# One chunk table changed: when the second weight is loaded, summed and rounded, and when three activations are queued, in a linear-attention block with a gated feed-forward

## The chip, the cores and the metric

The kernel is one program on one core of a Trainium2 chip. Its engines are TensorE (PE in the profile; PEld is its loading of weights), VectorE (DVE), ScalarE (ACT), GpSimd (POOL) and SyncE (SP), whose queue issues every DMA that is spoken of here. The metric is the device time of one execution in microseconds (us). Before the change it is 1128.17 us, the median of three runs (1127.15 to 1129.49).

## The reference, cut to what matters

```python
xn = layernorm(x)                       # x: 2048 x 576, float32
q, k, v = split(xn @ wqkv)              # 32 heads of 18
s = linear_attention(phi(q), phi(k), v) @ wo
h = gelu(xn @ w1 + b1)                  # w1: 576 x 4608
g = silu(h @ w2 + b2)                   # w2: 4608 x 576
out = x + s * g
```

## The kernel before, in words

Every float32 matmul is done with pairs: an operand is rounded to a short form (`hi`, a CAST on ScalarE), and what the rounding lost is kept beside it (`lo`, a subtraction on VectorE); three matmuls, hi by hi, hi by lo and lo by hi, make one product. The two matmuls of the feed-forward are besides done with seven products of blocks where eight would be plain (a Strassen-Winograd scheme), so that weights and activations first have sums made of their quarter blocks, and then those sums are rounded.

Attention takes the first 283 us or so and is not touched. The feed-forward runs over two halves of the rows (`half`), each over nine chunks of 512 columns of the hidden layer (`c`; `step` counts the 18 chunks). **A chunk has 28 steps** (`NS`). Steps 0 to 6 and 7 to 13 are the seven products of two `Up` objects: x by the first weight, in the order 1, 2, 6, 5, 7, 3, 4 (`UP`). Steps 14 to 27 are the seven products by the second weight, in the order 1, 2, 7, 4, 5, 3, 6 (`ORDER`), two steps each. In the first half of the rows every chunk prepares its weights while TensorE works, and stores them to DRAM; the second half loads them ready. The last chunk is done plainly.

TensorE, VectorE, ScalarE and GpSimd run the feed-forward strictly in the order in which it is written (`in_order`), SP's queue is placed by the scheduler. What is written where is set by tables: `add(base + k, f)` puts work behind step k of a chunk, `at_step` calls it there.

- **`P1` and `P0`** are the steps for the first weight of the chunk's second `Up` (steps of its own chunk) and of the next chunk's first `Up` (steps of the chunk before). `T` are GpSimd's sums in the raw weight (lines 800 to 807, tile `w1raw`), `hi` the roundings (line 811) and `lo` what is left (line 816), for the tiles `wa`, `w` (product 6), `wc` and `wd`.
- **`PW2`** is the same for the second weight: `T` are the four sums 5, 7, 6, 4 in the raw tile `w2raw` (line 1151), `hi` and `lo` the seven operands (lines 754 and 757, tiles `w2_...`, printed by the profile as `w__` and a number). Sum 5 overwrites the block that operand 1 reads, sum 6 the one of operand 3, and sum 4 the one of operand 2, so each comes behind those roundings.
- **`load_raw`** (line 609) loads the next chunk's raw second weight into the one `w2raw` buffer.
- **`Up.step`**: bank `a` is written by product 1, read by a ScalarE copy into `mid` (line 1107), then added to by product 6, read again (line 1114), added to by product 7. TensorE therefore waits at step 2 and step 9 for the copy of line 1107, and at step 4 and step 11 for that of line 1114. VectorE's additions are on lines 1110 to 1129, the gelu on line 1098.
- **`silu_first`** (line 1309) applies silu to a finished block of the first half of the rows, in place in `macc`, and stores it (`c_dram`); the blocks C12, C21 and C22 are queued at steps 0 and 1 of the first chunk of the second half, behind the additions `combine` (line 1249).

Of the kernel before, what the change touches and what calls it, by code (L numbers as in the profile page):

```python
# [44 lines left out]
def linear_attention_gated_ffn(ctx, tc, x, xT, wqkv, wo, w1, w1e, b1, w2, b2, out):  # L45
# [733 lines left out]
    class W1:  # L779
# [11 lines left out]

        def T(self, i):


            a, b = slice(0, 2), slice(2, 4)
            f0, f1, src = self.f0, self.f1, self.src
            tt = EW1.tensor_tensor
            if i == 5:
                src[5] = f0[:, a]
                tt(src[5], f1[:, a], f0[:, a], op=SUB)  # L800
            elif i == 6:
                src[6] = w1p.tile([P, 2, P], F32, tag="w1t6", name="w1t6", bufs=1)
# [153 lines left out]
    def beside(i, k):  # L956
# [14 lines left out]
        else:  # L971
# [91 lines left out]
    C11, C12, C21, C22, U1 = range(5)  # L1063
# [69 lines left out]
    class W2:  # L1133
# [9 lines left out]

        def T(self, i):
            src = self.src
# [22 lines left out]
        def load(self, i):  # L1168
            t, self.ops[i] = op_tile(fr, [2, HD], f"w2_{i}", 1, f"w2_{self.n}_")
            nc.sync.dma_start(t.bitcast(F32), w2_dram[self.n % NC, i])  # L1170

    class HOps:
# [6 lines left out]
        def add(self, pr, g):  # L1179
            for (par, b), t in g.items():  # L1180
                self.A[pr, b, par] = t
                self.src[{(0, 0): 1, (0, 1): 2, (1, 1): 4, (1, 0): "-"}[b, par], pr] = t
# [218 lines left out]
    NS = 28  # L1401

    def plan_w1(add, w, base, T, hi, lo):
        for table, what in ((T, w.T), (hi, w.hi), (lo, w.lo)):
            for i, at in table.items():
                add(base + at, what, i)

    P1 = dict(  # L1410
        T={5: 1, 6: 1, 7: 1, 4: 2},
        hi={"a": 0, 6: 2, "c": 3, "d": 4},
        lo={"a": 0, 6: 3, "c": 4, "d": 5},
    )
    P0 = dict(
        T={5: 24, 6: 24, 7: 25, 4: 25},
        hi={"a": 21, 6: 25, "c": 26, "d": 27},
        lo={"a": 22, 6: 25, "c": 26, "d": 27},
    )


    PW2 = dict(
        T={5: 3, 7: 3, 6: 4, 4: 4},
        hi={2: 0, 1: 1, 3: 2, 7: 5, 4: 6, 5: 8, 6: 9},
        lo={2: 1, 1: 2, 3: 3, 7: 6, 4: 7, 5: 9, 6: 10},
    )
    W2_NEXT = {1: 15, 2: 17, 7: 19, 4: 21, 5: 23, 3: 25, 6: 27}
    PH = dict(
        S={(7, 0): 7, (5, 0): 8, (6, 0): 11, (3, 0): 11, (7, 1): 13, (5, 1): 14, (6, 1): 15, (3, 1): 15},
        hi={  # L1430
            (1, 0): 7, (2, 0): 9, (7, 0): 10, (1, 1): 11, (2, 1): 12, (7, 1): 15, (4, 0): 16,
            (4, 1): 17, (5, 1): 18, (5, 0): 19, (6, 0): 20, (3, 0): 21, (3, 1): 22, (6, 1): 23,
        },
        lo={
            (1, 0): 10, (2, 0): 10, (7, 0): 11, (1, 1): 12, (2, 1): 13, (7, 1): 15, (4, 0): 16,
            (4, 1): 17, (5, 1): 18, (5, 0): 19, (6, 0): 20, (3, 0): 21, (3, 1): 22, (6, 1): 23,
        },
# [22 lines left out]
    for step in range(n_chunks):  # L1460
        half, c = divmod(step, NC)
        base = step * NS
        plain = step == n_chunks - 1
        h = HOps(c)
        if half == 0:
            plan_w1(add, w1t[2 * step + 1], base, **P1)
            for what in ("T", "hi", "lo"):
                for i, at in PW2[what].items():
                    add(base + at, getattr(w2t[step], what), i)
        change = step == NC - 1  # L1470
        if not plain:
            add(base + (11 if change else 7), load_we, 2 * step + 2)
            add(base + (16 if change else 14), load_we, 2 * step + 3)
        if half == 0 and c < NC - 1:
            add(base + 0, make, W1, w1t, 2 * step + 2)
            add(base + 4, make, W1, w1t, 2 * step + 3)
            add(base + 1, lambda n=2 * step + 2, base=base: plan_w1(add, w1t[n], base, **P0))
            make(W2, w2t, step + 1)
            add(base + 22, w2t[step + 1].load_raw)
        elif not plain:  # L1480
            add(base + (11 if change else 7), make, W1Loaded, w1t, 2 * step + 2)
            add(base + (11 if change else 14), load_six, 2 * step + 2)
            add(base + (16 if change else 14), make, W1Loaded, w1t, 2 * step + 3)
            if step + 2 < n_chunks:
                make(W2, w2t, step + 1)
                for i, at in W2_NEXT.items():
                    add(base + at + 10 * change, lambda i=i, n=step + 1: w2t[n].load(i))
            else:
                make(W2, w2t, step + 1)

                w = w2t[step + 1]
                add(base + 7, w.load_raw)
                for f in range(CF):
                    add(base + 22 + f, lambda f=f, w=w: (w.plain(f), w.hi(("p", f))))
                    add(base + 24 + f, w.lo, ("p", f))
        if not plain:
            if half == 0 and c == NC - 1:
                for k, at in X_AT.items():
                    add(base + at, load_x_part, k)
                add(base + 14, lambda: x_new.update(rs=load_rests(0)))  # L1500
                add(base + 25, silu_first, C11)
                for k in range(2):
                    add(base + 26 + k, combine, C12, nc.vector, slice(2 * k, 2 * k + 2))
                    add(base + 26 + k, combine, C21, nc.gpsimd, slice(2 * k, 2 * k + 2))
            for what in ("S", "hi", "lo"):
                for (i, pr), at in PH[what].items():
                    add(base + at, getattr(h, what), i, pr)
        if half == 1 and c == 0:
            add(base, silu_first, C12)
            add(base, silu_first, C21)  # L1510
            add(base, combine, C22, nc.vector, slice(0, 2))
            add(base + 1, combine, C22, nc.vector, slice(2, 4))
            add(base + 1, silu_first, C22)
        if half == 1 and c:
            for k in range(2):
                tiles = {}
                def load(k=k, t=7 + c, tiles=tiles):
                    tiles[0] = finish_tiles(k)
                    finish_load(t, k, tiles[0])
                add(base, load)  # L1520
                add(base + 4, lambda k=k, t=7 + c, tiles=tiles: finish(t, k, tiles[0]))
        if plain:
            for m in (C12, C21, C22):
                add(base + 4, combine, m, nc.gpsimd)
            for t, at in enumerate((6, 7, 12, 13, 5, 12, 12, 12)):
                add(base + at, load_xs, t)
            for b, f, at, lo in (
                (0, 0, 7, 8), (0, 1, 8, 9), (1, 0, 10, 10), (1, 1, 10, 11), (0, 2, 11, 12),
                (0, 3, 12, 13), (1, 3, 13, 13), (1, 2, 13, 13),
            ):  # L1530
# [68 lines left out]
```

## Time and profile before

| | us |
|---|---|
| runs before, median of 3 | 1128.17 |
| the profiled execution | 1128.05 |
| its span, first to last instruction | 1126.3 |
| attention, to the start of the feed-forward | 282.66 |
| first half of the rows, first chunk's `Up` | 24.60 |
| the eight chunk lengths from 307.26 to 689.46 | 382.20 |
| first half to second half, 689.46 to 738.80 | 49.34 |
| a chunk of the second half | 44.65 |

The page's first part gives the busy time of the engines, the fourth the chain of work that ended last. A stretch by stage (busy time of each engine, with the clock granted to TensorE as PEclk) and a timeline of instructions (start, length, engine, line, tiles, and in brackets the idle time ahead with what ended it) are the other two views used below.

### The profile page before, as it was taken

What the parts mean: (1) busy time and instruction counts of PE and PEld (TensorE: products, weight loads), DVE (VectorE), ACT (ScalarE), POOL (GpSimd) and SP (SyncE); (2) the same over time, 40 slices, a digit from 0 to 9 for tenths busy, and PEclk for the clock granted to TensorE, in tenths of its full rate; (3) what the DMA queues carried; (4) which work ended last, traced back from release to release, by engine and by line L of the source; (5) the groups of instructions that cost most, each with busy time, mean ns of one, the idle gap of its engine ahead of it and who ended that gap; (6) DMA issues with size and microseconds to landing.
All of it is one profiled execution on the core that took longest, in us unless ns stands there. A gap on an engine that the chain in (4) does not pass through costs nothing.

```text
span 1126.3 us, 18080 instructions
## 1 busy us (share of the span) xinstructions
PE 1098.3 (98%) x6702; PEld 1012.0 (90%) x6702; DVE 774.1 (69%) x1096; ACT 551.5 (49%) x954; POOL 461.9 (41%) x394
## 2 busy tenths in 40 slices
PE   9999999999999999999999999899999999999998
PEld 8999989999798897988879798798998998989988
DVE  7655348787788787888778887474574664745756
ACT  6454355555745556464554645544244253352542
POOL 3433224333646546375463745224232242241340
PEclk9999999999999999999999999999999999999999
DMA  6864224675947648375583839978676767766452
GB/s 209 212 149 125 72 84 152 200 260 185 365 172 269 228 182 312 145 304 200 192 302 151 327 133 354 377 269 273 215 228 220 248 205 226 222 226 209 144 189 86
DMA packets 84224, 242.78 MB, mean 216 GB/s; under 512 B 11430, under 2 KB 23718, under 8 KB 81448
## 3 DMA queue, kind: packets, MB, share of 16 engines
q1 hardware_dynamic: 84136, 241.62, 63.0%
q8 instruction: 53, 0.87, 0.3%
q14 instruction: 35, 0.29, 0.1%
HBM read 145.66 MB, written 93.99 MB: 213 GB/s over the span
## 4 chain that ended last, share of the span: by engine, by line
PE 87%; POOL 5%; issue 2%; ACT 2%; DVE 2%; DMA 1%; SPq 0%; POOLq 0%; ACTq 0%; DVEq 0%
PE pm L1233 34%; PE a L1090 12%; PE e L1090 8%; PE bc L1090 6%; PE pk L320 6%; PE pq L320 5%; PE ps_s L730 5%; PE pv L320 4%; POOL w2raw L1151 4%; PE pd L1349 2%; PE ps_kva L381 1%; DMA op_c<-wc 1%; PE ptp L712 1%; POOL w1t L803 1%; DMA b2b<-b 1%
## 5 line engine op out<-in xcount | busy, mean ns | idle before, releaser
L1239 DVE TENSOR_TENSOR macc<-pm,macc 128x576 f32<-128x576 f32 x218 | 164.6, 755 | 62.6 <-PE pm L1233 61.3
L754 ACT CAST h_h<-g 128x512 fp32r<-128x512 f32 x204 | 122.9, 620 | 136.3 <-PE pm L1233 135.3
L757 DVE TENSOR_TENSOR h_l<-g,h_h 128x512 fp32r<-128x512 f32 x204 | 157.9, 778 | 11.8 <-ACT h_h L754 11.5
L1199 POOL TENSOR_TENSOR mid<-g 128x512 f32<-128x512 f32 x34 | 44.1, 1296 | 107.3 <-ACT g L1098 107.2
L1098 ACT ACTIVATE g<-bc,b1c 128x512 f32<-128x512 f32 x72 | 49.6, 689 | 55.9 <-DVE bc L1110 39.3
L1193 POOL TENSOR_TENSOR g<-g 128x512 f32<-128x512 f32 x34 | 52.3, 1538 | 39.8 <-ACT h_h L754 20.2
L1107 ACT COPY mid<-a 128x512 f32<-128x512 f32 x36 | 21.1, 585 | 95.2 <-PE a L1090 94.0
L800 POOL TENSOR_TENSOR w1raw<-w1raw 128x256 f32<-128x256 f32 x18 | 13.3, 738 | 130.6 <-ACT h_h L754 68.9
L1151 POOL TENSOR_TENSOR w2raw<-w2raw 128x576 f32<-128x576 f32 x36 | 65.2, 1810 | 2.1
L1120 DVE TENSOR_TENSOR z<-a,mid 128x512 f32<-128x512 f32 x36 | 25.0, 695 | 51.0 <-PE a L1090 51.0
L1196 POOL TENSOR_TENSOR g<-g 128x512 f32<-128x512 f32 x34 | 52.6, 1548 | 7.6 <-DVE h_l L757 5.5
L1321 POOL TENSOR_TENSOR fin1l<-fin1h,fin1l 128x288 f32<-128x288 f32 x8 | 7.0, 878 | 118.7 <-DMA fin1l<-s_dram 56.9
L1110 DVE TENSOR_TENSOR bc<-bc,mid 128x512 f32<-128x512 f32 x36 | 25.0, 694 | 41.7 <-PE bc L1090 39.8
L1090 PE MATMUL a<-s,w 128*128 128x512 f32 x108 | 32.1, 438 | 17.5 <-ACT mid L1107 17.5
L1190 POOL TENSOR_TENSOR g<-g 128x512 f32<-128x512 f32 x34 | 47.5, 1398 | 2.7
L1121 ACT COPY mid<-a 128x512 f32<-128x512 f32 x36 | 21.1, 587 | 50.0 <-DVE z L1120 50.0
L695 POOL TENSOR_TENSOR pbuf<-phiq,den 128x576 f32<-128x576 f32 x16 | 19.4, 1212 | 63.6 <-DVE den L694 63.6
L1090 PEld LDWEIGHTS a<-s,w 128*128 128x128 f32 x108 | 21.6, 207 | 25.6 <-ACT mid L1107 21.3
L320 PE MATMUL pk<-wkv_h,xh 128*128 128x288 f32 (+1 forms) x160 | 38.2, 321 | 0.4 <-ACT xh L247 0.4
L320 PE MATMUL pk<-wkv_l,xh 128*128 128x288 f32 (+1 forms) x160 | 38.2, 321 | 0.0
L339 DVE SCALAR_TENSOR_TENSOR phik<-pk,ek 128x576 f32<-128x576 f32 x16 | 12.1, 758 | 37.0 <-ACT ek L337 37.0
L730 PE MATMUL ps_s<-kw_h,th 128*128 128x288 f32 x160 | 35.5, 303 | 0.0
(894 smaller groups left out, 3671.1 us busy)
## 6 DMA issues: line engine op xcount, KB each, us to landing
we<-we_dram SPq DMA_DIRECT2D x36, 448.0 KB
w2raw<-w SPq DMA_DIRECT2D x10, 1152.0 KB
w1raw<-w SPq DMA_DIRECT2D x18, 512.0 KB
op_a<-wa SPq DMA_DIRECT2D x18, 512.0 KB
op_c<-wc SPq DMA_DIRECT2D x18, 512.0 KB
op_d<-wd SPq DMA_DIRECT2D x18, 512.0 KB
wc<-op_c SPq DMA_DIRECT2D x18, 512.0 KB
wa<-op_a SPq DMA_DIRECT2D x18, 512.0 KB
```

Source lines behind the costliest of these rows:

```text
L320: nc.tensor.matmul(ps[:, h, : ws.stop - ws.start], st, w[:, k, ws], start=(begin and i == 0), stop=(end and i == len(seq) - 1), skip_group ...
L730: nc.tensor.matmul(ps[:, h, :HD], st[:, k, :], w[:, k, h * HD : (h + 1) * HD], start=(i == 0), stop=(i == len(seq) - 1),)
L754: nc.scalar.copy(pair[0], src)
L757: eng.tensor_tensor(pair[1], src, pair[0].bitcast(F32), op=SUB)
L1090: nc.tensor.matmul(ps, st, mv, start=first and n == 0, stop=n == len(seq) - 1, skip_group_check=True,)
L1098: nc.scalar.activation(g, ps, AF.Gelu_apprx_tanh, bias=b1c[:, f : f + 1])
L1151: tt(dst, a, b, op=SUB)
L1190: tt(src[5, pr], A(1, 0), A(1, 1), op=ADD)
L1193: tt(src[6, pr], src[5, pr], A(0, 0), op=SUB)
L1196: tt(src[3, pr], A(0, 1), src[6, pr], op=SUB)
L1233: nc.tensor.matmul(ps[:, q, :HD], hs[p][st][:, cs], m[:, p, :], start=(n == 0 and i not in CHAIN), stop=(n == 5), skip_group_check=True,)
L1239: nc.vector.tensor_tensor(dst, src, dst, op=ADD)
```

## The change

`P1`, `P0` and `PW2` get other step numbers; `PW2` may now hold negative ones, which are steps at the end of the chunk before, and a new function `plan_w2` queues those from the chunk before; the load of the next raw second weight is queued at step 16 instead of 22; and the three `silu_first` are queued together behind step 13 of their chunk.

```diff
     P1 = dict(
-        T={5: 1, 6: 1, 7: 1, 4: 2},
-        hi={"a": 0, 6: 2, "c": 3, "d": 4},
-        lo={"a": 0, 6: 3, "c": 4, "d": 5},
+        T={5: 1, 6: 1, 7: 3, 4: 3},
+        hi={"a": 0, 6: 4, "c": 7, "d": 7},
+        lo={"a": 0, 6: 5, "c": 8, "d": 8},
     )
     P0 = dict(
-        T={5: 24, 6: 24, 7: 25, 4: 25},
+        T={5: 18, 6: 18, 7: 19, 4: 19},
...
     PW2 = dict(
-        T={5: 3, 7: 3, 6: 4, 4: 4},
+        T={5: -1, 7: 2, 6: 2, 4: 4},
...
+    def plan_w2(n, ahead):
+        for what in ("hi", "lo", "T"):
+            for i, at in PW2[what].items():
+                if (at < 0) == ahead:
+                    add(max(n * NS + at, 0), getattr(w2t[n], what), i)
...
-            add(base + 22, w2t[step + 1].load_raw)
+            add(base + 16, w2t[step + 1].load_raw)
+            plan_w2(step + 1, True)
...
         if half == 1 and c == 0:
-            add(base, silu_first, C12)
-            add(base, silu_first, C21)
             add(base, combine, C22, nc.vector, slice(0, 2))
             add(base + 1, combine, C22, nc.vector, slice(2, 4))
-            add(base + 1, silu_first, C22)
+            for m in (C22, C21, C12):
+                add(base + 13, silu_first, m)
```

GpSimd, in the `Up` of the chunk with raw weights `w1raw6`, `w1raw7` and `w2raw3` (one chunk of the first half; the others read alike). Before:

```order
L807 TENSOR_TENSOR w1raw6_4219<-w1raw6_4219,w1t6_4631 128x256
L800 TENSOR_TENSOR w1raw7_4292<-w1raw7_4292 128x256
L803 TENSOR_TENSOR w1t6_4723<-w1raw7_4292 128x256
L805 TENSOR_TENSOR w1raw7_4292<-w1raw7_4292 128x256
L807 TENSOR_TENSOR w1raw7_4292<-w1raw7_4292,w1t6_4723 128x256
L1151 TENSOR_TENSOR w2raw3_4590<-w2raw3_4590 128x576 x4
```

With the change:

```order
L807 TENSOR_TENSOR w1raw6_4230<-w1raw6_4230,w1t6_4530 128x256
L1151 TENSOR_TENSOR w2raw3_4483<-w2raw3_4483 128x576
L800 TENSOR_TENSOR w1raw7_4287<-w1raw7_4287 128x256
L803 TENSOR_TENSOR w1t6_4734<-w1raw7_4287 128x256
L1151 TENSOR_TENSOR w2raw3_4483<-w2raw3_4483 128x576 x2
L805 TENSOR_TENSOR w1raw7_4287<-w1raw7_4287 128x256
L807 TENSOR_TENSOR w1raw7_4287<-w1raw7_4287,w1t6_4734 128x256
L1151 TENSOR_TENSOR w2raw3_4483<-w2raw3_4483 128x576
```

The first sum of the second weight stands ahead of all of `w1raw7`, two more stand amid them, and only the last is still at the end.

VectorE, from the last addition of a chunk's products (line 1239) to the addition of product 2 in the next (line 1110). Before:

```order
L1239 TENSOR_TENSOR macc_3214<-pm6_4672,macc_3214 128x2x288
L816 TENSOR_TENSOR wd_6_4686<-w1raw6_4219,wd_6_4686 128x512
L816 TENSOR_TENSOR wa_7_4703<-w1raw7_4292,wa_7_4703 128x512
L1110 TENSOR_TENSOR bc6_4693<-bc6_4693,mid_3217 128x512
L757 TENSOR_TENSOR w2_3__4708<-w2raw3_4590,w2_3__4708 128x576
```

With the change:

```order
L1239 TENSOR_TENSOR macc_3214<-pm6_4674,macc_3214 128x2x288
L757 TENSOR_TENSOR w2_3__4669<-w2raw3_4483,w2_3__4669 128x576
L816 TENSOR_TENSOR wd_6_4694<-w1raw6_4230,wd_6_4694 128x512
L816 TENSOR_TENSOR wa_7_4711<-w1raw7_4287,wa_7_4711 128x512
L757 TENSOR_TENSOR w2_3__4688<-w2raw3_4483,w2_3__4688 128x576
L1110 TENSOR_TENSOR bc6_4698<-bc6_4698,mid_3217 128x512
```

Two subtractions of the second weight, those of operands 1 and 3, now stand ahead of the addition of line 1110.

ScalarE, from the gelu of step 6 to that of step 8. Before:

```order
L754 CAST w2_3__4798<-w2raw3_4590 128x576
L1098 ACTIVATE g_4808<-bc6_4693,b1c_78 128x512
L754 CAST w2_3__4810<-w2raw3_4590 128x576
L1107 COPY mid_3217<-a7_4815 128x512
L754 CAST h10_h_4833<-g_4720 128x512
L1098 ACTIVATE g_4844<-bc7_4817,b1c_78 128x512
```

With the change:

```order
L754 CAST w2_3__4793<-w2raw3_4483 128x576
L1098 ACTIVATE g_4803<-bc6_4698,b1c_78 128x512
L754 CAST w2_3__4805<-w2raw3_4483 128x576
L1107 COPY mid_3217<-a7_4810 128x512
L811 CAST wc_7_4822<-w1raw7_4287 128x512
L811 CAST wd_7_4824<-w1raw7_4287 128x512
L754 CAST h10_h_4832<-g_4731 128x512
L1098 ACTIVATE g_4843<-bc7_4812,b1c_78 128x512
```

The rounding just ahead of the copy of line 1107 reads GpSimd's last sum (4) before, and the last but one (6) with the change; the two roundings of `wc` and `wd`, which stood at steps 3 and 4, follow the copy, and their subtractions on VectorE (line 816) follow the addition of step 8.

More of the change, by code (lines that the diff above doesn't have):

```diff
@@ L1410, in linear_attention_gated_ffn @@
     P1 = dict(
-        T={5: 1, 6: 1, 7: 1, 4: 2},
-        hi={"a": 0, 6: 2, "c": 3, "d": 4},
-        lo={"a": 0, 6: 3, "c": 4, "d": 5},
+        T={5: 1, 6: 1, 7: 3, 4: 3},
+        hi={"a": 0, 6: 4, "c": 7, "d": 7},
+        lo={"a": 0, 6: 5, "c": 8, "d": 8},
     )
     P0 = dict(
-        T={5: 24, 6: 24, 7: 25, 4: 25},
-        hi={"a": 21, 6: 25, "c": 26, "d": 27},
-        lo={"a": 22, 6: 25, "c": 26, "d": 27},
+        T={5: 18, 6: 18, 7: 19, 4: 19},
+        hi={"a": 16, 6: 23, "c": 25, "d": 27},
+        lo={"a": 17, 6: 24, "c": 26, "d": 28},
     )
     PW2 = dict(
-        T={5: 3, 7: 3, 6: 4, 4: 4},
-        hi={2: 0, 1: 1, 3: 2, 7: 5, 4: 6, 5: 8, 6: 9},
-        lo={2: 1, 1: 2, 3: 3, 7: 6, 4: 7, 5: 9, 6: 10},
-    )
+        T={5: -1, 7: 2, 6: 2, 4: 4},
+        hi={1: -2, 3: -1, 2: 0, 5: 2, 7: 5, 6: 6, 4: 9},
+        lo={1: -1, 3: 0, 2: 1, 5: 3, 7: 6, 6: 7, 4: 10},
+    )
+    def plan_w2(n, ahead):
[3 more added lines that the diff above has]
+                    add(max(n * NS + at, 0), getattr(w2t[n], what), i)
     W2_NEXT = {1: 15, 2: 17, 7: 19, 4: 21, 5: 23, 3: 25, 6: 27}
@@ L1466, in linear_attention_gated_ffn @@
             plan_w1(add, w1t[2 * step + 1], base, **P1)
-            for what in ("T", "hi", "lo"):
-                for i, at in PW2[what].items():
-                    add(base + at, getattr(w2t[step], what), i)
+            if step == 0:
+                plan_w2(0, True)
+            plan_w2(step, False)
         change = step == NC - 1
```

## The prediction

> **What bounds the kernel now.** I first read the busy times and the shares of the chain that ended last.
>
> ```profile
> span 1126.3 us, 18080 instructions
> ...
> PE 1098.3 (98%) x6702; PEld 1012.0 (90%) x6702; DVE 774.1 (69%) x1096; ACT 551.5 (49%) x954; POOL 461.9 (41%) x394
> ...
> PE 87%; POOL 5%; issue 2%; ACT 2%; DVE 2%; DMA 1%; SPq 0%; POOLq 0%; ACTq 0%; DVEq 0%
> ```
>
> TensorE sets the end; the change leaves its matmuls alone, so all that can be won is its waiting. Where that lies is read from the stretches, cut at step 14 of a chunk, in order: first chunk's `Up`, eight chunk lengths of the first half, the passage to the second half, one undisturbed chunk, then one chunk of each of the two kinds in the first half and one microsecond of the first of them.
>
> ```profile
> core 0: us, PE busy (x) PEld busy (x) DVE busy (x) ACT busy (x) POOL busy (x), PEclk, DMA share, GB/s
> 282.66:307.26 24.60, 23.28 (x102) 18.29 (x101) 18.83 (x22) 18.24 (x32) 16.94 (x12) 1.00 0.99 378
> 307.26:689.46 382.20, 365.70 (x2131) 329.20 (x2130) 308.13 (x409) 205.85 (x362) 211.73 (x161) 0.99 0.61 227
> 689.46:738.80 49.34, 46.34 (x269) 41.76 (x268) 30.14 (x41) 27.17 (x39) 14.92 (x10) 0.97 0.95 372
> 738.80:783.45 44.65, 44.65 (x269) 40.78 (x268) 25.87 (x37) 17.80 (x31) 14.19 (x12) 1.00 0.79 272
> 401.84:450.62 48.78, 46.75 (x269) 41.90 (x268) 38.73 (x52) 26.05 (x47) 26.55 (x21) 0.97 0.61 226
> 450.62:497.64 47.02, 44.96 (x269) 40.70 (x268) 37.80 (x52) 25.33 (x45) 26.29 (x20) 1.00 0.62 233
> 441.00:442.00 1.00, 1.00 (x3) 0.82 (x3) 1.00 (x2) 0.26 (x1) 1.00 (x1) 0.50 1.02 419
> ```
>
> A chunk in which TensorE never waits takes 44.65, or 44.65 / 28 = 1.595 a step. Eight such would be 357.2; the first half takes 382.20, **25.0 too much, 3.1 a chunk**. The passage has 4.7 too much, the first `Up` 24.60 − 14 × 1.595 = 2.3. These 32 us are all that the change can win. Now the wait itself, from the table of waits and the timeline of the chunk that starts at 424.27:
>
> ```profile
> PE a L1090 <- ACT mid L1107: 17.5, 9, 2.1
> ```
>
> ```profile
> 432.05 7.50 POOL L1151 TENSOR_TENSOR w2raw<-w2raw 128x576 f32<-128x576 f32 x4
> ...
> 439.59 0.67 ACT L754 CAST w__4810<-w2raw 128x576 fp32r<-128x576 f32 x1 [1.87 <-POOL w2raw L1151]
> ...
> 440.17 0.58 ACT L1107 COPY mid<-a 128x512 f32<-128x512 f32 x1
> ...
> 440.80 0.67 PE L1090 MATMUL a<-s,w 128*128 128x512 f32 x1 [2.03 <-ACT mid L1107]
> ```
>
> TensorE stands 2.03 at step 9 for the copy, which is queued behind a rounding that waits for GpSimd's fourth sum of the second weight, at 439.55. Eight of the nine waits are this one, each about 2.05. Behind it comes a tail: the chunk without a lower clock has 47.02 − 44.65 = 2.37, so 0.3 of restart; the other has 1.8 more, and its clock row reads 0.50. Four of the eight are of that kind.
>
> A page's rule bears on that clock. The Trainium skill, "TensorE: Matmul & The Clock Gate", section "Part 1: The HAM clock gate", has the half clock after at least one idle window of about 3.4 us; by it, gaps under 2 us would cost themselves alone. Here a gap of 2.03 already stood before the 0.50, so the measurement decides against a firm limit of 3.4. By the rule the four tails of 1.8 would not be there to win, and no short new gap could bring the half clock; by the trace both can be.
>
> **The load at step 16.** SP issues it by its own queue:
>
> ```profile
> 402.49 0.55 SPq L609 DMA_DIRECT2D w2raw<-w  x1
> ```
>
> That is 22 us ahead of the chunk that uses it, and the order with the change has it in the same place of SP's queue, right behind the load of `we`. Its first reader is now a rounding queued at step −2, 19 us after the issue. I put it at 0; were it late by all that the DMA engines still have queued, it would show as a wait of ScalarE, for which no row speaks.
>
> **GpSimd alternates.** With sum 5 done early, the chain of sums that ended at 439.55 ends some 7.50 / 4 = 1.9 sooner, at 13.4 counted from the chunk's start instead of 15.3. The rounding ahead of the copy now reads sum 6, done by about 10. So the wait of 2.05, its restart and its clock go: the whole 3.1 a chunk. What is late next are VectorE's and ScalarE's moved roundings.
>
> ```profile
> 424.27 0.40 PE L1090 MATMUL a<-xh,wa 128*128 128x512 f32 x1
> ...
> 424.47 0.76 DVE L1239 TENSOR_TENSOR macc<-pm,macc 128x576 f32<-128x576 f32 x1 [0.24 <-PE pm L1233]
> ...
> 427.23 0.69 DVE L816 TENSOR_TENSOR wa<-w1raw,wa 128x512 fp32r<-128x512 f32 x1 [1.41 <-ACT wa L811]
> ...
> 427.84 0.69 DVE L1110 TENSOR_TENSOR bc<-bc,mid 128x512 f32<-128x512 f32 x1
> ...
> 428.44 0.91 DVE L757 TENSOR_TENSOR w__4708<-w2raw,w__4708 128x576 fp32r<-128x576 f32 x1
> 428.57 0.69 ACT L1098 ACTIVATE g<-bc,b1c 128x512 f32<-128x512 f32 x1 [0.80 <-DVE bc L1110]
> ...
> 430.67 0.39 PE L1090 MATMUL a<-xh,wc 128*128 128x512 f32 x1
> ...
> 433.23 1.31 DVE L816 TENSOR_TENSOR wc<-w1raw,wc 128x512 fp32r<-128x512 f32 x1
> ...
> 436.91 1.38 DVE L757 TENSOR_TENSOR w__4798<-w2raw,w__4798 128x576 fp32r<-128x576 f32 x1
> ```
>
> **New wait at step 4** (times from 424.27). A subtraction of 576 columns takes 0.76 with GpSimd idle (as the addition at 424.47) and 1.38 beside line 1151 (436.91); one of 512 columns 0.69 (427.23) and 1.31 (433.23). Line 1239 ends at 0.96, the new subtraction of operand 1 at 1.64, and GpSimd's sum 5 runs from there to about 3.6. The subtraction of `wd` runs beside it, to 2.3 to 2.9, and hides ahead of that of `wa`, which cannot start before 2.96, where its rounding lets it. `wa` ends at 3.65 alone, 4.27 contended; sum 5 covers two thirds of it, so I take 3.95. Then operand 3, 0.91 as at 428.44, and line 1110 starts at 4.70 (consecutive instructions overlap by some 0.08, as 427.84 + 0.69 and 428.44 show) where it started at 3.57. From its start 0.73 go to the gelu, then gelu 0.69, copy 0.58, less one overlap, and 0.05 to TensorE: 1.97. So bank `a` is free for step 4's product 7 at 6.67, where 430.67 shows that step starting at 6.40: **a wait of about 0.3**. Bounds: all alone 0; all contended (4.27 and 1.38) 1.05.
>
> **New wait at step 10.** The subtractions of `wc` and `wd` now stand behind line 1110 of step 8, and product 5 needs `wd`'s in its third matmul. An undisturbed chunk shows the times there:
>
> ```profile
> 764.25 1.75 PE L1090 MATMUL a<-s2r,we 128*128 128x512 f32 x7
> ...
> 764.50 0.70 DVE L1110 TENSOR_TENSOR bc<-bc,mid 128x512 f32<-128x512 f32 x1 [2.52 <-PE bc L1090]
> ...
> 765.84 0.39 PE L1090 MATMUL e<-s1r,wd 128*128 128x512 f32 x1
> ```
>
> Step 9 starts at 764.25, step 10 at 765.84, its third matmul 2/7 of a step later at 766.30, which is 1.80 after line 1110's start. The two subtractions would be done 0.61 + 0.61 + 0.69 = 1.9 after that start alone, 0.61 + 1.23 + 1.31 = 3.15 contended. With a release of 0.05 the wait is 0.15 to 1.40. GpSimd's own sums of the second weight are over by 13.4, before this place at 14.5, and only its sums of activations may run, so I take 0.5, nearer to the uncontended end. The roundings of `wc` and `wd` themselves follow the copy, and hide while line 1110 runs.
>
> Together 0.3 + 0.5 + 0.1 for two short restarts = 0.9 a chunk, 7.2 in eight; the first half gains 25.0 − 7.2 = **17.8**. Of the first `Up` I count half of this wait, 0.5 (0 to 2.3):
>
> ```profile
> 298.64 0.73 PE L1090 MATMUL a<-s,w 128*128 128x512 f32 x2 [1.17 <-ACT mid L1107]
> ```
>
> For a rule against the change: the Trainium skill, "SBUF — State Buffer", section "Who interferes with whom", calls the port pair of VectorE and GpSimd an exclusive lock: the loser blocks for the winner's whole instruction. A subtraction that meets a running sum early would by it take up to 1.9 + 0.69 = 2.6, which leads to the third case below; the row at 433.23 has 1.31 with line 1151 beside it throughout, so the trace does not agree in full.
>
> **The silus.** They now follow step 13's last gelu instead of standing among the `Up`'s activations.
>
> ```profile
> 713.99 2.25 ACT L1309 ACTIVATE macc<-macc 128x1152 f32<-128x1152 f32 x2
> ...
> 718.26 1.28 ACT L1309 ACT_TABLE_LOAD   x1
> 719.55 1.16 ACT L1309 ACTIVATE macc<-macc 128x1152 f32<-128x1152 f32 x1
> ...
> 721.24 0.80 PE L1090 MATMUL a<-h1r,wc 128*128 128x512 f32 x1 [3.00 <-ACT mid L1114]
> ...
> 739.58 0.69 ACT L1098 ACTIVATE g<-bc,b1c 128x512 f32<-128x512 f32 x1 [0.18 <-DVE bc L1125]
> ```
>
> The wait of 3.00 and its tail, 4.7 in all, go. New: one table load 1.28 and three silus of 1.13 to 1.16 start when the gelu of 739.58 ends (0.8 + 0.7 = 1.5 after step 14's start) and hold ScalarE to 6.2; a rounding for product 7 follows, about 0.6, ready with VectorE's part near 6.9. Step 18 starts at 4 × 1.595 = 6.4: a wait of 0.55 (0 to 1.2). Gain **4.1**.
>
> One thing moves with it on SP's queue. `rxm` for the second half is waited for there:
>
> ```profile
> SPq L1310 <- DMA rxm<-rq_dram: 0.6, 1, 0.6
> ```
>
> ```profile
> 709.14 0.58 SPq L1170 DMA_DIRECT2D w__7631<-op  x1
> ...
> 713.08 0.39 PE L1090 MATMUL a<-rxm,we 128*128 128x512 f32 x1
> ```
>
> It lands near 709.14 + 0.58 + 0.6 = 710.3, 2.8 ahead of its use, in a stretch whose DMA share is 0.95. The new order puts two stores and two loads of 0.52 MB ahead of it; at 419 GB/s these are 5 us, part of which waits anyway. I bound its cost at 0 to 2 and take 0.
>
> **Sum.** 17.8 + 0.5 + 4.1 = 22.4. The profiled execution took 1128.05 (span 1126.3 and 1.75 around it), 0.1 below the median of 1128.17. 1128.05 − 22.4 = **1105.6**.
>
> **The rivals.** *No new wait:* line 1110 and `wd` find GpSimd idle; 0.1 a chunk: 24.2 + 0.5 + 4.7, or 1098.7. For it: the uncontended bounds are 0 and 0.15. *Fuller contention:* both waits near their bounds, 2.2 a chunk with restart, and 1.5 for `rxm`: gain 7.4 + 0.5 + 2.6, or 1117.5. For it: 1.31 and 1.38 above; against it: sum 5 ends at 3.6, before operand 3's subtraction. *The change doesn't do what it says:* sum 6 is late as well, the copy still stands, 3.1 a chunk remain; then only the silus gain, 1124. Against it: sum 6 would have to be 3.5 later than laid out. *Slower:* the two new gaps, at their bounds of 1.05 and 1.40, bring the half clock in every chunk, 1.55 more (1.8 was seen): 4.0 a chunk, 32 in all, 7.0 lost in the first half, 2 for `rxm`; 7.0 + 2 − 4.6 = 4.4 lost, 1132.4. It decides from (25.0 + 4.6) / 8 = 3.7 a chunk on. Against it: the gap of 1.17 at 298.64 is in a stretch whose clock is 1.00.
>
> **Chances.** Forecast 0.58 (1102 to 1110, a chunk's cost 0.4 to 1.5), no new wait 0.20, fuller contention 0.14 (1110 to 1121), not as it says 0.05, slower 0.03. About 0.2%, 2.3 us, is what a measurement of this kernel can tell from no change. Faster is the first three and most of the fourth, 0.95; same 0.02; slower 0.03. Range 1097 to 1118: it takes in no new wait and most of the contention, and leaves out 0.15.
>
> **What would show it.** Right: no wait of about 2 for line 1107 at step 9, GpSimd's last sum ended near 13.4, no 0.50 in the clock row, chunks of 45.3 to 46; short waits at step 4 for line 1114 and at step 10 for `wd` of line 816; 738.80 − 689.46 shrunk to 45.2. Wrong: a wait for `w2raw`'s load; an exclusive wait of 1.9 of VectorE; TensorE waiting for `rxm`; or a new wait behind step 14, where the rounded second weights are now made in another order.

## The result, and the profile after

The changed kernel takes 1114.52 us (median of four, 1113.47 to 1115.10) beside 1128.34 for the kernel before on the same chips: a ratio of 0.9877, 95% interval 0.9859 to 0.9894. It is faster by 13.8, where 22.4 was forecast; 1114.5 lies in the range. The profiled execution took 1114.99, 13.1 less than that of before. First the page's busy times:

```profile
span 1113.3 us, 18079 instructions
...
PE 1095.2 (98%) x6702; PEld 1007.4 (90%) x6702; DVE 773.9 (70%) x1096; ACT 547.8 (49%) x954; POOL 455.7 (41%) x394
```

Then four stretches, cut at the first matmul of step 14 (columns as before): the eight chunk lengths, the passage, the chunk behind it from step 14 to step 14, and last the `Up` of chunk 0:

```profile
307.86:678.09 370.23, 363.81 (x2129) 325.25 (x2128) 309.85 (x409) 201.31 (x361) 207.22 (x160) 1.00 0.64 237
678.09:724.13 46.04, 44.90 (x267) 40.71 (x266) 30.31 (x41) 21.72 (x34) 14.88 (x10) 1.00 0.98 386
724.13:770.22 46.09, 45.22 (x268) 40.88 (x266) 25.10 (x37) 23.43 (x36) 13.52 (x12) 1.00 0.84 306
282.61:307.86 25.25, 22.82 (x101) 18.25 (x99) 18.30 (x22) 18.52 (x32) 16.89 (x12) 1.00 0.79 291
```

The eight chunks gain 382.20 − 370.23 = 12.0 (17.8 forecast). The passage gains 3.3 and the chunk behind it loses 1.4, together 1.9 (4.1 forecast). The first `Up` loses 0.8 (a gain of 0.5 forecast): cut at the first matmul of step 14, as here, it was 24.44 before, for the cuts of the prediction all lie 0.16 behind that matmul. The clock column is 1.00 throughout: the half clock is gone. A chunk now takes 370.23 / 8 = 46.28, so 1.63 more than the undisturbed 44.65, and the table of waits names where:

```profile
PE e L1090 <- DVE wd L816: 7.8, 9, 1.8
...
PE a L1090 <- DMA rxm<-rq_dram: 1.1, 1, 1.1
PE a L1090 <- ACT mid L1114: 0.6, 1, 0.6
```

Line 1107 has left the table of TensorE's waits; in its place stands the wait at step 10 that the prediction named, for VectorE's `wd`. What made it longer than forecast is read from the timeline of the chunk that starts at 423.07, all engines together (the rows of steps 7 to 10 that matter):

```profile
436.27 1.45 POOL L1199 TENSOR_TENSOR mid<-g 128x512 f32<-128x512 f32 x1 [0.33 <-ACT g L1098]
...
436.79 1.55 DVE L757 TENSOR_TENSOR w__4805<-w2raw,w__4805 128x576 fp32r<-128x576 f32 x1 [0.23 <-ACT w__4805 L754]
...
437.80 1.70 POOL L1190 TENSOR_TENSOR g<-g 128x512 f32<-128x512 f32 x1
...
438.26 0.69 DVE L1110 TENSOR_TENSOR bc<-bc,mid 128x512 f32<-128x512 f32 x1
438.86 1.19 DVE L816 TENSOR_TENSOR wc<-w1raw,wc 128x512 fp32r<-128x512 f32 x1
...
439.97 0.68 DVE L816 TENSOR_TENSOR wd<-w1raw,wd 128x512 fp32r<-128x512 f32 x1
...
440.70 0.50 PE L1090 MATMUL e<-s,wd 128*128 128x512 f32 x1 [0.76 <-DVE wd L816]
```

GpSimd ends its last weight sum at 434.34 + 1.61 = 435.95, 12.9 of the chunk, even before the 13.4 forecast. It waits only 0.33 for a gelu then: the activation sums of lines 1199 and 1190, which in the profile before began at 439.52, 15.3 of its chunk, now begin at 13.2. The row of before:

```profile
439.52 1.26 POOL L1199 TENSOR_TENSOR mid<-g 128x512 f32<-128x512 f32 x1
```

The first of them meets the subtraction of operand 6 (1.55 for 0.76), the second that of `wc` (1.19 for 0.68). Line 1110, `wc` and `wd` stand in that queue, and the third matmul of step 10 comes at 440.70 instead of 439.33 + 0.46 = 439.79: 0.91 late, about 1.04 with the slower restart (its first matmul takes 0.50, the others 0.39). Of the 0.91, 0.26 is line 1110 itself: it starts 0.51 behind step 9's first matmul (437.75), in the undisturbed chunk 0.25, because operand 6's subtraction stands ahead of it. The other 0.65 is `wc` and `wd` behind it, 0.5 of it the slowed `wc`.

The ends of the slowed rows tell how GpSimd holds them up. The sum of line 1199 ends at 437.72 and operand 6's subtraction 0.62 later; that of line 1190 ends at 439.50 and `wc`'s 0.55 later. That is no accident of two rows: in the traces of before and after, 301 subtractions start inside a running sum, at least 0.15 ahead of its end, and every one ends 0.28, 0.55 or 0.61 behind the sum, to 0.01, for 256, 512 or 576 columns. The lag goes with the size and not with the overlap, which runs from 0.17 to 1.37; two engines that shared time would show less lag after more overlap. So **the subtraction does nothing until the sum ends**, and what it costs depends on when within the sum it starts, from nothing to the whole sum. The addition of line 1110, which reads the bank that TensorE wrote, is not held up: it runs inside the sum of line 1190 at 438.26 and keeps its 0.69.

Step 4 came as laid out: line 1110 started 4.67 into the chunk (4.70 forecast) and step 4 at 6.61 (6.67 forecast), 0.34 lost with its restart.

```profile
427.74 0.69 DVE L1110 TENSOR_TENSOR bc<-bc,mid 128x512 f32<-128x512 f32 x1
...
429.68 0.50 PE L1090 MATMUL a<-xh,wc 128*128 128x512 f32 x1
```

### The profile page after: what moved, and what is told of

It is laid out like the page before. It is cut to its first block, busy times and chain, and to the rows that moved or that the text cites. A ratio compares the mean times of both kernels' runs of the same rounds, so it can differ in the third digit from the quotient of the medians.

```text
span 1113.3 us, 18079 instructions
## 1 busy us (share of the span) xinstructions
PE 1095.2 (98%) x6702; PEld 1007.4 (90%) x6702; DVE 773.9 (70%) x1096; ACT 547.8 (49%) x954; POOL 455.7 (41%) x394
## 4 chain that ended last, share of the span: by engine, by line
PE 87%; ACT 4%; DVE 3%; DMA 3%; issue 2%; SPq 0%; POOL 0%; ACTq 0%; DVEq 0%; POOLq 0%
PE pm L1233 32%; PE a L1090 11%; PE e L1090 8%; PE bc L1090 7%; PE pk L320 6%; PE pq L320 5%; PE ps_s L730 5%; PE pv L320 4%; PE pd L1349 2%; DMA rxm<-rq_dram 1%; PE ps_kva L381 1%; DVE wc L816 1%; DMA we<-op 1%; PE ptp L712 1%; DVE wd L816 1%
## 5 line engine op out<-in xcount | busy, mean ns | idle before, releaser
L1151 POOL TENSOR_TENSOR w2raw<-w2raw 128x576 f32<-128x576 f32 x36 | 60.7, 1687 | 99.6 <-DVE w__5651 L757 11.5
L1193 POOL TENSOR_TENSOR g<-g 128x512 f32<-128x512 f32 x34 | 51.9, 1526 | 31.1 <-DVE h_l L757 29.8
L1196 POOL TENSOR_TENSOR g<-g 128x512 f32<-128x512 f32 x34 | 49.2, 1448 | 7.6 <-DVE h_l L757 5.5
L1190 POOL TENSOR_TENSOR g<-g 128x512 f32<-128x512 f32 x34 | 47.5, 1397 | 2.7
L1090 PE MATMUL e<-s,wd 128*128 128x512 f32 x108 | 30.0, 400 | 7.8 <-DVE wd L816 7.8
L1129 DVE TENSOR_TENSOR e<-e,mid 128x512 f32<-128x512 f32 x36 | 25.1, 696 | 16.8 <-PE e L1090 16.8
L320 PE MATMUL pq<-wq_h,xh 128*128 128x288 f32 x160 | 34.8, 299 | 0.0
```

The lines of the kernel that those rows point to most:

```text
L320: nc.tensor.matmul(ps[:, h, : ws.stop - ws.start], st, w[:, k, ws], start=(begin and i == 0), stop=(end and i == len(seq) - 1), skip_group ...
L1090: nc.tensor.matmul(ps, st, mv, start=first and n == 0, stop=n == len(seq) - 1, skip_group_check=True,)
L1151: tt(dst, a, b, op=SUB)
L1190: tt(src[5, pr], A(1, 0), A(1, 1), op=ADD)
L1193: tt(src[6, pr], src[5, pr], A(0, 0), op=SUB)
L1196: tt(src[3, pr], A(0, 1), src[6, pr], op=SUB)
```

## The experiments

"Chunk" below is the steady length from step 14 to step 14 in the first half, 46.28 with the change and 44.65 undisturbed; its first part are the `Up`s (23.66 and 22.26), its second the products (22.61 and 22.39). Most kernels had one execution beside one of the kernel before on the same chip; chunks repeat within 0.1 in a trace, but for those named, and the verdicts rest on them. The first `Up` does not repeat: it took 25.25 in five kernels and 26.9 in two in which nothing of it was changed (the last section says why), so a time may differ by 1.6 for that alone.

**The first weight's table undone.**

```diff
-        T={5: 1, 6: 1, 7: 3, 4: 3}, hi={"a": 0, 6: 4, "c": 7, "d": 7}, lo={"a": 0, 6: 5, "c": 8, "d": 8},
+        T={5: 1, 6: 1, 7: 1, 4: 2}, hi={"a": 0, 6: 2, "c": 3, "d": 4}, lo={"a": 0, 6: 3, "c": 4, "d": 5},
```

> The changed kernel with the second Up's table P1 of before (roundings of wc and wd at steps 3 and 4, their subtractions at 4 and 5); PW2, P0, the load and the silus stay changed. Theory: the wait for line 816 at step 10 (0.76 in the trace of the change, 1.04 with its restart) is caused by the subtraction of wd standing behind line 1110 of step 8. Then that wait goes in every chunk, the chunk length falls from 46.28 to 45.2 to 45.5, and the time to about 1106. Rival: those subtractions meet GpSimd's sums of the second weight at their earlier place (1.31 instead of 0.69), delay line 1125 and with it the copy of line 1107, and a wait of 0.5 to 1 stands at step 9 in its place: chunk 46 or more, time 1112 to 1115.

1113.13 (before: 1129.71), chunk 46.27. The wait at step 10 went and the `Up`s fell to 23.00, but the products rose to 23.25: neither theory had that. The waits of its trace (whole program behind 300 us) and the rows at the new place:

```profile
PE pm L1233 <- ACT h_h L754: 5.6, 9, 0.7
```

```profile
454.88 0.68 DVE L816 TENSOR_TENSOR wa<-w1raw,wa 128x512 fp32r<-128x512 f32 x1
455.48 0.75 DVE L1239 TENSOR_TENSOR macc<-pm,macc 128x576 f32<-128x576 f32 x1
```

Product 4 adds into the bank of product 7, which this addition of line 1239 must have read. It ends at 456.23, and TensorE, waiting since 455.7, starts at 456.37. The table puts the wait down to a rounding of ScalarE that ends then, and the next run tells them apart.

**Both tables of the first weight undone.** As above, and `P0` of before too.

> The changed kernel with both tables of the first weight, P1 and P0, as before; only PW2 (with its GpSimd alternation), the load and the silus stay changed. Theory: with P1 back alone, the wait of 0.65 in the products, 10.4 us behind step 14, is VectorE being late: its addition of step 18 (line 1239) stands behind P0's early subtraction of wa (step 17) and behind subtractions slowed by GpSimd, and product 4 adds into the bank that this addition reads. With P0 back that subtraction moves to step 22, the products fall from 23.25 to 22.4 to 22.8 while the Up stays at 23.0, so a chunk is 45.4 to 45.8 and the time 1107 to 1111. Rival: the wait belongs to ScalarE's roundings (as the table of waits names it) and stays at 0.4 or more.

1108.35 (before: 1129.93); chunk 45.66, `Up`s 23.01, products 22.66. In its trace ScalarE's two roundings are still running when TensorE starts product 4 at 408.31, and VectorE's addition ended 0.15 earlier:

```profile
407.42 0.74 DVE L1239 TENSOR_TENSOR macc<-pm,macc 128x576 f32<-128x576 f32 x1
...
407.77 1.14 ACT L754 CAST h_h<-g 128x512 fp32r<-128x512 f32 x2 [2.06 <-PE pm L1233]
...
408.31 0.37 PE L1233 MATMUL pm<-w__4369,h_h 128*128 128x288 f32 x1
```

So the wait belongs to VectorE, late from the `Up`, and the early subtraction of `wa` in the new `P0` made it longer. The two new tables of the first weight thus cost 0.62 a chunk together (46.28 against 45.66): of the three tables, only the second weight's gains. **`P0` alone undone** says the same:

```diff
-        T={5: 18, 6: 18, 7: 19, 4: 19}, hi={"a": 16, 6: 23, "c": 25, "d": 27}, lo={"a": 17, 6: 24, "c": 26, "d": 28},
+        T={5: 24, 6: 24, 7: 25, 4: 25}, hi={"a": 21, 6: 25, "c": 26, "d": 27}, lo={"a": 22, 6: 25, "c": 26, "d": 27},
```

> The changed kernel with table P0 of before (the next chunk's first Up prepared at steps 21 to 27 instead of 16 to 28). Theory: P0 itself matters little in the steady chunks (46.1 to 46.6), and the wait of 1.14 for rxm at the passage falls under 0.3, because the stores of the last raw chunk's wc and wd move in SP's queue with P0. Rival: the sums of GpSimd for the next chunk at steps 24 and 25 meet its sum 5 of the second weight at step -1, VectorE's start of the next Up is later, and the chunk is 46.8 or more.

1113.20 (before: 1129.38); chunk 46.05 and products 22.38, so `P0` costs the changed kernel 0.23 a chunk (and 0.6 with `P1` of before). The expected end of the wait for `rxm` was a miss: 1.13 stayed.

**GpSimd's activation sums cut short.**

```diff
-                tt(src[5, pr], A(1, 0), A(1, 1), op=ADD)
+                cut = slice(0, 64 if 0 < self.c < NC - 1 and pr == 0 else 512)
+                tt(src[5, pr][:, cut], A(1, 0)[:, cut], A(1, 1)[:, cut], op=ADD)
...
-                tt(src[7, pr], A(0, 0), A(1, 0), op=SUB)
+                tt(src[7, pr][:, cut], A(0, 0)[:, cut], A(1, 0)[:, cut], op=SUB)
```

> The changed kernel in which GpSimd sums only 64 of 512 columns of the activation operands 7 and 5 of a chunk's first pair (lines 1199 and 1190), in chunks 1 to 7 of either half; the rest of those two operands is left unsummed. Theory: GpSimd, free earlier, now runs these sums at 13.2 to 16.4 of a chunk beside VectorE's subtractions of operand 6 (1.55 instead of 0.75) and of wc (1.19 instead of 0.68), which is what made the wait at step 10 1.04 instead of the 0.5 forecast. Then with the sums cut these two take about 0.75 and 0.69, and the wait at step 10 falls to 0.1 to 0.3, the chunk from 46.28 to about 45.5. Rival: the place behind line 1110 alone makes the wait; the durations stay or do not matter, and the chunk stays above 46.0.

1110.36 (before: 1129.71), chunk 45.50 (46.29 for the last of the eight, whose sums are whole), and the table has no wait of matmuls for `wd` left in the chunks with cut sums. VectorE's rows there:

```profile
436.54 0.76 DVE L757 TENSOR_TENSOR w__4805<-w2raw,w__4805 128x576 fp32r<-128x576 f32 x1 [0.21 <-ACT w__4805 L754]
437.76 0.70 DVE L1110 TENSOR_TENSOR bc<-bc,mid 128x512 f32<-128x512 f32 x1 [0.46 <-PE bc L1090]
438.37 0.68 DVE L816 TENSOR_TENSOR wc<-w1raw,wc 128x512 fp32r<-128x512 f32 x1
438.96 0.69 DVE L816 TENSOR_TENSOR wd<-w1raw,wd 128x512 fp32r<-128x512 f32 x1
```

Same queue, same place behind line 1110, and each row at its own length: the collision was worth 0.8 of the 1.04. Step 10 still takes 1.88 where an undisturbed step takes 1.59; these 0.3 are the place itself.

**Operand 3's subtraction behind line 1110.**

```diff
-        lo={1: -1, 3: 0, 2: 1, 5: 3, 7: 6, 6: 7, 4: 10},
+        lo={1: -1, 2: 1, 3: 1, 5: 3, 7: 6, 6: 7, 4: 10},
```

> The changed kernel with the subtraction of operand 3 of the second weight queued at step 1 (behind line 1110) instead of step 0. Theory: it is what stands ahead of line 1110 and holds step 4 for 0.3; then the idle time of TensorE's weight loads for line 1114 at step 4 goes, and the chunk falls by 0.3 to about 46.0 (2.5 us in all, time about 1112). Rival: step 10's wait is set by VectorE and GpSimd on their own clock and takes back what step 4 gives: the chunk stays within 0.1 of 46.28.

1115.00 (before: 1129.71), chunk 46.30: the rival. Its table of waits, of which 1.8 is the first `Up`:

```profile
PE e L1090 <- DVE wd L816: 10.7, 9, 1.8
```

Step 4 no longer waits, and the wait at step 10 grew from 0.75 to 1.11, by all that step 4 had given. Over these steps VectorE and GpSimd keep a pace of their own, and TensorE's earlier arrival only lengthens its wait.

**`wc` and `wd` ahead of line 1110.** With `P0` of before (chunk 46.05):

```diff
-        lo={"a": 0, 6: 5, "c": 8, "d": 8},
+        lo={"a": 0, 6: 5, "c": 7, "d": 7},
...
-        lo={1: -1, 3: 0, 2: 1, 5: 3, 7: 6, 6: 7, 4: 10},
+        lo={1: -1, 3: 0, 2: 1, 5: 3, 7: 6, 6: 10, 4: 10},
```

> The changed kernel with P0 of before, with the subtractions of wc and wd queued at step 7 (ahead of line 1110 of step 8) instead of step 8, and with that of operand 6 of the second weight at step 10 instead of 7. Theory: at step 10 it is VectorE's order that counts; without the subtraction of operand 6 (1.55) ahead of them the two are done at 16.6 of a chunk, before TensorE needs wd at 16.7, and line 1110 follows at 16.5, so that step 11 waits 0.2 to 0.4 for line 1114: Up 22.7 to 23.0, products 22.4, chunk 45.1 to 45.4, time 1104 to 1108. Rival: line 1110, now later, costs step 11 as much as step 10 gains: Up 23.4 or more.

1116.94 (before: 1129.93), chunk 46.63: a miss, the rival and more. The rows of GpSimd and of VectorE:

```profile
438.82 1.85 POOL L1190 TENSOR_TENSOR g<-g 128x512 f32<-128x512 f32 x1
```

```profile
438.82 0.69 DVE L816 TENSOR_TENSOR wc<-w1raw,wc 128x512 fp32r<-128x512 f32 x1 [1.23 <-ACT wc L811]
439.43 1.78 DVE L816 TENSOR_TENSOR wd<-w1raw,wd 128x512 fp32r<-128x512 f32 x1
441.14 0.69 DVE L1110 TENSOR_TENSOR bc<-bc,mid 128x512 f32<-128x512 f32 x1
```

`wc` and the sum start at once, `wc` runs first, and the sum ends at 440.67; `wd`, ready at 439.43, ends 0.54 behind it. The expected 0.69 for `wd` became 1.78, ahead of line 1110.

**The load at step 22 again.**

```diff
-            add(base + 16, w2t[step + 1].load_raw)
+            add(base + 22, w2t[step + 1].load_raw)
```

> The changed kernel with the raw second weight's load queued at step 22 instead of 16. Theory: SP issues it by its own queue and this edit is worth nothing: chunk 46.28 and time 1114.5 within 0.1 per chunk and 1.5 in all. Rival: the new early roundings (steps -2 and -1) need it earlier, and ScalarE waits for w2raw, with a chunk over 46.6.

1113.95 (before: 1129.38), chunk 46.29: the earlier load is worth nothing. This trace has no wait for `rxm`, though its chunk 8 is queued as in the changed kernel.

**The silus back at steps 0, 0 and 1**, and **the silus at steps 13, 15 and 17**:

```diff
-            for m in (C22, C21, C12):
-                add(base + 13, silu_first, m)
+            for m, at in ((C22, 13), (C21, 15), (C12, 17)):
+                add(base + at, silu_first, m)
```

> The changed kernel with the silus back at steps 0, 0 and 1 of that chunk. Theory: the wait of 3.0 for line 1114 in its Up comes back (Up 26.0 to 27 instead of 23.65), the products fall from 23.83 to 22.4, so the silu part of the change was worth 1.7 to 3; the wait for rxm (1.14) stays, since it belongs to the moved loads and stores. Rival: the wait for rxm goes, and the silu part is worth less than 1.5.

> The changed kernel with the three silus at steps 13 (C22), 15 (C21) and 17 (C12) of the first chunk of the second half instead of all at 13. Theory: one table load and three silus back to back hold ScalarE from 725.77 to 730.3 in the trace of the change, so the rounding for product 7 and those behind it come late: waits of 0.41 and 0.45, and 23.83 for the products of that chunk where an undisturbed one takes 22.39. With one silu ahead of that rounding and the others behind later ones the products take 22.4 to 22.7 and the time falls by 1.1 to 1.4. Rival: the loss there is from VectorE or from the stores of the blocks, which product 7 waits for as it writes C22: then the products stay above 23.4.

Back: 1118.77 (before: 1129.38). The wait for line 1114 is 2.98 again; passage and next chunk take 51.44 + 44.65 = 96.09 where the change has 46.04 + 46.09 = 92.13. The silu part is worth 4.0 here, more than expected: the `Up` took 29.05, the products fell to 22.38 as expected, and of the wait for `rxm` 0.44 stayed. But a good part of the 4.0 is clock, which is 0.89 in the stretch from 699 to 729 of that trace. With the silus in the same place that `Up` takes 26.95 in the kernel before (3.41 us of half clock) and 25.55, at full clock, in the run with operands 4 and 6 exchanged below.

Spread: 1119.59 (before: 1129.38), the rival, and worse; 1.6 of it is the first `Up`. Products of that chunk took 28.17, passage and chunk 44.65 + 50.43 = 95.08. VectorE's row:

```profile
742.20 0.76 DVE L1243 TENSOR_TENSOR macc<-pm,b2b 128x576 f32<-128x576 f32 x1 [6.03 <-DMA c_dram<-macc]
```

A later silu makes a later store of the block, which stands behind loads in SP's queue, and the addition that overwrites the block waits 6.03 for it, TensorE behind it 3.58.

**Before, with operands 4 and 6 exchanged.** What of the alternation frees the copy: GpSimd's earlier end, or only that another operand is rounded ahead of it?

```diff
-        hi={2: 0, 1: 1, 3: 2, 7: 5, 4: 6, 5: 8, 6: 9}, lo={2: 1, 1: 2, 3: 3, 7: 6, 4: 7, 5: 9, 6: 10},
+        hi={2: 0, 1: 1, 3: 2, 7: 5, 6: 6, 5: 8, 4: 9}, lo={2: 1, 1: 2, 3: 3, 7: 6, 6: 7, 5: 9, 4: 10},
```

> The kernel of before with one thing changed: the rounding and the subtraction of operand 6 of the second weight at steps 6 and 7, those of operand 4 at 9 and 10 (they were the other way round). GpSimd's sums stay back to back. Theory: what freed the copy of line 1107 is that the rounding ahead of it no longer reads GpSimd's last sum; the third sum ended at 437.75 in a chunk that starts at 424.27, so the copy could end at 438.9 where TensorE needs it at 438.6: the wait at step 9 falls from 2.05 to 0.3 to 0.5, the half clock goes, the chunk falls to 45.2 to 45.6, time 1108 to 1112 with the passage of 49.34 as before. Rival: it is the alternation on GpSimd, which ends 1.9 sooner, that is needed; then 1 or more of the wait stays and the time is above 1117.

1113.17 (before: 1129.71), chunk 46.05: as much as the whole change, from one exchange and with GpSimd's sums back to back.

```profile
PE a L1090 <- ACT mid L1114: 5.0, 10, 3.0
PE pm L1233 <- ACT h_h L754: 1.4, 8, 0.2
PE a L1090 <- ACT mid L1107: 1.4, 8, 0.2
```

The step 9 wait is down from 2.05 to 0.2; the chunk stays over the 45.2 to 45.6 expected, as waits of 0.2 at step 11 and in the products came up.

**Before, with operand 6 behind the copy.** The same with operand 6 rounded at step 7 and subtracted at step 10.

> The kernel of before with the rounding of operand 6 of the second weight at step 7 and its subtraction at 10, that of operand 4 at 9 and 10; GpSimd's eight sums stay back to back, and the silus at 0, 0 and 1. Theory: the alternation on GpSimd is not needed at all: with no rounding of a GpSimd sum ahead of the copy but that of operand 7, step 9 does not wait, and the chunk is 44.8 to 45.2, as in the best version; time 1105 to 1108, since the passage stays at 48 to 49. Rival: sums that end 1.9 later push GpSimd's activation sums and VectorE's subtractions behind them, and the waits of 0.2 at step 11 and in the products stay or grow: chunk 45.5 or more, time 1109 or more.

1114.25 (before: 1132.39), chunk 46.10 (the first 45.06): the rival. One chunk, its `Up`s and its products:

```profile
421.04:443.30 22.26, 22.26 (x100) 18.39 (x99) 18.25 (x22) 15.05 (x28) 16.00 (x12) 1.00 0.95 359
443.30:467.14 23.84, 23.00 (x170) 22.47 (x168) 21.07 (x30) 10.44 (x18) 10.63 (x9) 1.00 0.33 126
```

The `Up`s are without any wait, and the products pay 1.45. The chain of work there goes through VectorE:

```profile
438.32 1.85 DVE w__4825 L757
440.17 0.18 DVE w__4854 L757
...
440.76 1.28 DVE h_l L757 x2
442.05 0.62 DVE z L1120
...
444.42 1.59 PE pm L1233 x9
```

Operand 6's subtraction meets line 1190 and takes 1.85; what is behind it on VectorE is late up to the roundings that step 14 needs. So the wait at step 9 is not all: with the eight sums back to back, the activation sums behind them meet other subtractions. The best version below, which has the alternation, pays nothing in the products; as it differs in the second weight's other places too, this does not show that the alternation alone is what helps.

**A version that beats both.** Both first-weight tables of before, `PW2` with the alternation, operand 6 behind the copy, operand 3 behind line 1110, one silu early:

```diff
-        hi={1: -2, 3: -1, 2: 0, 5: 2, 7: 5, 6: 6, 4: 9}, lo={1: -1, 3: 0, 2: 1, 5: 3, 7: 6, 6: 7, 4: 10},
+        hi={1: -2, 3: -1, 2: 0, 5: 2, 7: 5, 6: 7, 4: 9}, lo={1: -1, 2: 1, 3: 1, 5: 3, 7: 6, 6: 10, 4: 10},
...
-            for m in (C22, C21, C12):
+            add(base, silu_first, C12)
+            for m in (C22, C21):
```

> The kernel with P1 and P0 as before (chunk 45.66) and three more places: the rounding of operand 6 of the second weight at step 7, behind the copy of line 1107 instead of ahead of it, its subtraction at 10 instead of 7; the subtraction of operand 3 at step 1, behind line 1110; and the silu of C12 at step 0 of its chunk instead of 13. Theory: step 4 waits 0.3 for what stands ahead of line 1110, step 9 0.25 for the one rounding (0.56) ahead of the copy; only when both go does the chunk gain, by 0.4 to 0.6, to 45.05 to 45.3; the silu shortens ScalarE's block behind step 13 by 1.1 and the products of that chunk from 23.84 to 22.8 to 23.3, at no wait in its Up. Time 1103 to 1105.5. Rival: VectorE's subtractions wait for GpSimd on GpSimd's clock, so the copy of line 1107, behind the gelu of line 1125's sum, is no earlier, and step 9 takes back what step 4 gives: chunk 45.5 or more, time 1107 or more.

1099.92 (median of four, 1099.68 to 1100.27), ratio to before 0.9745, interval 0.9729 to 0.9762: better than expected. A chunk, `Up`s and products, then the chunk behind the passage:

```profile
418.78:441.23 22.45, 22.45 (x101) 18.31 (x100) 19.71 (x24) 15.55 (x28) 17.72 (x12) 1.00 0.96 367
441.23:463.62 22.39, 22.39 (x170) 22.39 (x169) 19.22 (x28) 9.72 (x18) 9.05 (x8) 1.00 0.32 122
709.97:755.23 45.26, 44.87 (x267) 40.80 (x266) 25.33 (x37) 22.36 (x35) 13.96 (x12) 1.00 0.79 288
```

44.8 a chunk, 0.2 over the undisturbed, though VectorE is as busy as before; the passage takes 44.65, with no wait at all. Step 4 takes its 1.59 again and step 9 waits less, 0.17 with its restart where both tables undone leave 0.34. That operand 3's move, which gave nothing by itself, gives something beside operand 6's is the likely reading; neither move was run alone on this kernel, so how the 0.85 a chunk splits stays open.

## Why the prediction was right, and where not

- **The bound and the freed wait: right.** Line 1107's eight waits, their restarts and the half clock went. But the reason was too broad. It gave two causes, GpSimd's end 1.9 sooner and a rounding of sum 6 ahead of the copy; the second is enough (2.05 to 0.2 by the exchange of operands 4 and 6 alone).
- **The count of half clocks: wrong, and without effect on the sum.** Three of the eight chunks have it (48.78, 48.77 and 48.83, the others 47.0 to 47.3), not four; the fourth stretch of half clock is in the passage. The sum goes by the total of 25.0.
- **Load at step 16, at 0: right** (46.29 against 46.28).
- **Step 4, 0.3: right** to 0.1, and so are its rows but for two that offset each other: `wa` ended 0.13 later than taken, operand 3's subtraction was 0.17 shorter.
- **Step 10: right in place and mechanism, mis-sized.** The term "I take 0.5, nearer to the uncontended end" measured 0.91, and 1.04 with its restart. The step that failed is the argument "only its sums of activations may run": they were seen and priced as if they came late, while the freed GpSimd began them at once. Nor had the sum a term for line 1110 coming late itself, 0.26. With the activation sums cut short 0.3 of the 1.04 is left.
- **A chunk's cost of 0.9 was 1.63.** By position: step 4 0.34, step 10 1.04, products 0.22, the rest 0.03. The forecast had no term for the products. Six of the eight chunks before lost as much there: that of 47.26 had 24.62 and 22.64, against 22.26 and 22.39 undisturbed, and the forecast credited all of the 3.1 to the wait of step 9. With the change the loss hangs on the first weight's tables: 22.38 with `P0` of before, 23.25 with `P1` of before. The difference, 0.73 eight times, is 5.8 of the 9.3 missing.
- **First `Up`:** 1.3 of the miss. The gain of 0.5 became a loss of 0.8, with a wait of 1.80 at its step 10; with the half clock, which two other kernels had there, it would have been 2.5.
- **Silus, 4.1: near the 4.0 by undoing it, and by luck.** The `Up` gave 5.4 there (29.05 against 23.65) where 4.7 was forecast, by twice the half clock, and the products cost 1.44, not 0.55: there were two waits, 0.45 and 0.41, behind the silus instead of one. The stretch gained 1.9, so 2.2 is missing: 0.9 by the products, the rest by the wait for `rxm`, taken at 0 and bounded by 2: 1.14, and 1.39 with its restart (23.65 against 22.26).
- **What the wait for `rxm` hangs on** can be read from the kept traces: when SP issues that load. It did so 8.6 us behind step 14 in the changed kernel and in that with `P0` undone (waits of 1.14 and 1.13), 8.1 with the sums cut (0.59), 7.6 in two more (0.44 and 0.16), and 3.3 to 7.5 in all others, which do not wait. With `P1` of before it is 5.3 or less. Why SP comes to it between 6.9 and 8.6 in kernels whose queue is alike there stays open.
- **The rule weighed and put aside.** The prediction read 1.31 under line 1151 as less than a lock. It is one. The chain of waits of the kernel before gives the ends of the sums singly:

```profile
435.91 1.77 POOL w2raw L1151
```

This sum ended at 437.68, and the subtraction of 436.91, 1.38 long, at 438.29, 0.61 behind it. So the 1.31 beside line 1151, which the prediction held against the rule, is what the rule gives. The Trainium skill, "SBUF — State Buffer", section "Who interferes with whom", has the loser block for the whole instruction; the ends here (0.54 to 0.62 behind GpSimd's, four rows in three kernels) agree with it. Durations alone hid it, since a subtraction that starts late in a sum loses little.

## What to carry to other kernels

When an engine is freed early, list what it will start next and whom that meets; here it began its next sums 2 us sooner, in front of the very subtractions that had just been moved there. A wait for the last of several results is cured first by waiting for another of them; only then is it worth making the last one earlier. Where one busy pair of engines sets two waits in turn, taking away the first alone can only move it to the second, as step 4's 0.34 came back whole at step 10.

## What the runs showed of the hardware, not expected

VectorE's subtraction and GpSimd's sum do not share time: whichever is second waits for the other to end. In the rows of 438.82 of `wc` and line 1190, which start within 0.01, VectorE keeps its 0.69 and GpSimd's sum takes 1.85; a sum of that line takes 1.30 at 444.40 of the best version. In two other chunks of the kernel of that row, the one with `wc` and `wd` ahead (345.53 and 392.18), the subtraction starts 0.01 behind the sum; there it takes 1.83 and the sum 1.29.

And the clock: the length of a gap does not decide alone. The gap of 1.80 in the first `Up` left the clock at 1.00 in the changed kernel; in the run with the sums cut and in that with the silus spread the same gap was followed by 3.41 us of 0.50 (from 302.42 and 302.49), and the `Up` took 26.9. The stretches of half clock begin on a grid: in the trace before at 440.96, 536.54, 679.90 and 720.86, which are 28, 42 and 12 times 3.413 apart. Extended over each trace from its last stretch of half clock, this grid of cells of 3.413 us sorts every gap of over 0.9 us of the feed-forward in all fourteen traces. Where one cell of the grid held 1.80 or more of a gap, the half clock began with the next cell (nine gaps, the least 1.80, 1.81 and 1.99); where no cell held more than 1.77, it did not. So the gap of 2.06 that ends at 632.39 (1.77 and 0.28 in two cells) cost nothing more, nor did one of 3.00 in the kernel before with operands 4 and 6 exchanged (1.66 and 1.34), while one of 3.00 in the kernel before with operand 6 behind the copy lay in one cell and was followed by it. In this case a gap of about 2 thus costs some 1.6 more, or nothing, by where it falls on the grid.
